# Attention and a shrink layer on one core: output turned by PE transposes, the band mask as a sum in PSUM, DMA turns from pair 10, and a re-costed planner

## The chip, the cores and the metric

The kernel runs on one core of one Trainium2 chip. The metric is device time in microseconds (us) of one execution; the kernel before has a median of 334.55 us over 13 runs, from 331.03 to 338.65 us. The engines are PE (TensorE: matmuls, with its weight loads shown as PEld), DVE (VectorE), ACT (ScalarE), POOL (GpSimd) and SP (SyncE, which here only issues DMAs). Each engine executes its own instructions in the order in which they were emitted, and waits at an instruction whose inputs are not there.

## The reference

Inputs are q, k and v of shape (batch 8, heads 8, sequence 576, depth 64) and two weights, w_in (512 x 2048) and w_out (2048 x 512). For each batch and head two attentions are added:

```
local: softmax(q k^T / 8, only where |i - j| < 4) v
pooled: q, k, v averaged over groups of 4 tokens (144 groups),
        softmax(qd kd^T / 8) vd, each row repeated 4 times
x = (local + pooled), heads joined: 4608 tokens x 512
h = x w_in;  g = h - tanh(h);  out = g w_out
```

## The kernel before

**Attention by pairs.** The 64 (batch, head) items are taken two heads at a time: 32 pairs, four pairs (NP = 4) to a batch. A pair's q and k come by DMA into `qkn` (four buffers), v windows into `vst`. They are cast to bf16 and interleaved into `qr` (L515, L523), and turned so that depth lies on the partitions, into `qk`. Up to pair 11 the turn is nine PE transposes (L547) with copies out of PSUM (L551); from pair 12 (`T_DMA`) it is one DMA transpose `qT<-qr` (L531) and an ACT copy (L534). Pooled q and k are sums of four columns (`half` L564, `qkd` L569). From pair 12 (`NEW`) pooled v comes from its own load `v4` and two POOL sums (L472, L476); before that from PE (L492, L494).

**Scores and band.** The local scores are computed in windows: a tile of 120 queries against the 128 keys around it, four tiles and a last one of 96, so that a pair has 2 x 480 scores in one two-bank PSUM piece `t1` (L584), and 2 x 96 plus the pooled scores (L606) in another, `t2`. ACT takes the exponentials into `E` (L622, L634, L637). For pairs 0 to 3 PE adds a bias of -32768 outside the band before the scores (L589). For pairs 4 to 31 DVE multiplies the exponentials in SBUF by a 0/1 `mask` (L626 for 960 columns, L641 for 192). Then PE multiplies by v (L650, L657; a column of ones gives the sums), and DVE normalises into `ln` (L670, L672): seven blocks of up to 128 rows, five local and two pooled.

**Turn of the output.** `ln` must be turned so that heads lie on partitions, and pooled rows repeated 4 times. Up to pair 11 PE does both in one sum (`back`, L683 to L692): matmuls of the pooled blocks with a 0/1 matrix `up` and of the local blocks with the identity, into two PSUM banks, copied to `xT` by DVE (L720) or ACT (L721). From pair 12 (`X_DMA`) one DMA transpose `lT<-ln` (L696) turns it, and DVE or POOL (`join`, L703 and L709) adds local and repeated pooled part in SBUF.

**Dense part.** The 4608 tokens are nine blocks of 512. For each, `mm1` makes 16 tiles of h (L734, 4 matmuls of 512 columns each), ACT takes tanh (L742) and DVE subtracts (L745) into `gT`; `mm2` makes four tiles of the output (L760, 16 matmuls each), ACT copies them to `y` (L771) and SP stores them (L774). Block b needs all pairs of the batches that its tokens lie in.

**What sets the order.** A planner inside the kernel (`Program`) writes the order out. Each operation is entered with an engine, or several to choose from, a cost in ns, what it reads and writes, and a priority. `order` plays a list schedule with these costs: the engines, a latency `LAT` after each, 16 DMA queues as one resource, and eight PSUM banks with a cap for each kind of use (`P.cap`: attention "b" 6 banks, dense "d" 4). The instructions are then emitted in the order of the starts found, so the costs decide which instruction stands behind which on each engine. The chip waits only for data; where `after=` names a key, it is a dependence of the planner's order alone. `load_next` issues the loads of pair p + 4 in step p.

Of the kernel before, what the change touches and what calls it, by code (L numbers as in the profile page):

```python
# [23 lines left out]
class Program:  # L24

    LAT = {"PE": 270, "ACT": 150, "DVE": 110, "POOL": 150, "SP": 50, "DMA": 2200}
    RING = 230

    def __init__(self):
        self.ops = []  # L30
        self.alternatives = {}
        self.slack = []
        self.soon = set()
        self.goal = set()
        self.ring = {}
        self.rings = {}
        self.touch = []
        self.use = []
        self.toks = []
        self.cap = {}  # L40
        self.last_write = {}
        self.readers = {}
# [66 lines left out]
    def order(self):  # L109
# [56 lines left out]
        for i in range(n):  # L166
            if left[i] == 0:
                make_ready(i)
        for step in range(n):
            best = None  # L170
            for eng, cand in ready.items():
                if not cand:
                    continue
                now = max(free.get(eng, 0.0), min(at[i] for i in cand))
                if eng == "PE":
# [8 lines left out]
                else:  # L184
                    pick = min((self.ops[i][4], i) for i in cand if at[i] <= now)[1]
# [12 lines left out]
            end = now + self.ops[i][1]  # L198
            want = [t for t in self.use[i] if t.first == i]
# [57 lines left out]
def kernel(  # L257
# [41 lines left out]
    mask = fixed("mask", [128, 576], BF16)  # L299
# [19 lines left out]
    up = lT[1].rearrange("p n c -> p (n c)")[:, 0:S]  # L319
    r = fixed("r", [128, 2, 7], FP32, 2)  # L320
    ln = fixed("ln", [128, 7, 128], BF16, 2)
# [31 lines left out]
    def c_up():  # L353

        GP.memset(up, 1.0)
        GP.affine_select(out=up, in_=up, compare_op=ALU.is_ge, fill=0.0,
                         base=0, pattern=[[1, S]], channel_multiplier=-4)
        GP.affine_select(out=up, in_=up, compare_op=ALU.is_ge, fill=0.0,
                         base=3, pattern=[[-1, S]], channel_multiplier=4)

# [8 lines left out]
    def c_mask():  # L369

        GP.memset(mask, 1.0)
        m4 = mask[:, 0:480].rearrange("p (t c) -> p t c", c=QW)
        for part, pat in ((m4, [[0, 4], [1, QW]]),
                          (mask[:, 480:576], [[1, 96]])):
            neg = [[-s, n] for s, n in pat]
            GP.affine_select(
                out=part, in_=part, compare_op=ALU.is_ge, fill=0.0,
                base=-1, pattern=neg, channel_multiplier=1)
            GP.affine_select(
                out=part, in_=part, compare_op=ALU.is_ge, fill=0.0,  # L380
                base=7, pattern=pat, channel_multiplier=-1)
        GP.affine_select(
            out=mask[:, 0:QW], in_=mask[:, 0:QW], compare_op=ALU.is_ge,
            fill=0.0, base=-4, pattern=[[0, QW]], channel_multiplier=1)
        GP.affine_select(
            out=mask[:, 480:576], in_=mask[:, 480:576], compare_op=ALU.is_ge,
            fill=0.0, base=99, pattern=[[0, 96]], channel_multiplier=-1)
# [6 lines left out]
    def load_qk(p):  # L394

        b, h0, s = p // NP, 2 * (p % NP), p % NQKN
        for i, src in enumerate((q, k)):
# [6 lines left out]
            load(600, issue, [("qkn", s, i)], T_QK, 380, -30, 8, (), eng)  # L404
# [63 lines left out]
    def pool_v4(p):  # L468
# [9 lines left out]
        op("POOL", 1150, a1, reads=[("v4", s)], writes=["v2"], pri=10 * p - 12)  # L478
        op("POOL", 750, a2, reads=["v2"], writes=[("vp", s)], pri=10 * p - 12)

    def pool_v(hb):
# [15 lines left out]
        op("ACT", 590, lambda: A.copy(  # L497
# [5 lines left out]
    def attention(p):  # L503
# [10 lines left out]
        if p >= NEARLY:  # L514
            op("POOL", 1300, lambda: GP.tensor_copy(  # L515
# [14 lines left out]
        if p >= T_DMA:  # L530
            P.dma("SP", 1740, lambda: nc.sync.dma_start_transpose(  # L531
                out=qT[s], in_=qr[s].rearrange("p a c -> p (a c)")), 1300, 72,
                  src=[("qr", s, 0), ("qr", s, 1)], dst=[("qT", s)], pri=-50, lead=500)
            op("ACT", 1250, lambda: A.copy(  # L534
# [3 lines left out]
        else:  # L538
            for a0, a1, tn, cn in ((0, 5, 290, 740), (5, 9, 230, 620)):
# [10 lines left out]
                def copy(fn, a0=a0, a1=a1, b16=b16):  # L550
# [5 lines left out]
                          ("DVE", cn, lambda copy=copy: copy(V.tensor_copy))][:1 + (p < NP)],  # L556
# [10 lines left out]
        def add2(eng):  # L567
            with nc.allow_low_precision("pooled q and k"):
                eng.tensor_tensor(out=qkd[s][:, 0:G],  # L569
                                  in0=half[:, :, 0, :],  # L570
                                  in1=half[:, :, 1, :], op=ALU.add)
        P.choice([(name, n1, lambda eng=eng: add1(eng)) for name, n1, _, eng in adders],
# [41 lines left out]
        if new:  # L614
            op("PE", 620, s12, slack=late, reads=qks + [("qkd", s)], fill=[t1, t2], pri=pri)
        else:
            op("PE", 420 * cold + 250 * (p < NP), s1, slack=late,
# [4 lines left out]
        op("ACT", 960, lambda: A.activation(  # L622
            out=e1, in_=two(t1)[:, :, 0:480], func=AF.Exp, scale=SCALE),
           drain=[t1], writes=[("E", e, 0)], pri=pri)
        if p >= NP:
            op("DVE", 950, lambda: V.tensor_tensor(  # L626
                out=e1, in0=e1,
                in1=mask[:, 0:480].unsqueeze(1).to_broadcast([128, 2, 480]),
                op=ALU.mult), reads=["mask"], writes=[("E", e, 0)], pri=pri)
        yield  # L630
        if not new:
            op("PE", 380 * cold + 100 * (p < NP), s2, slack=late, reads=qks + [("qkd", s)],
               fill=[t2], pri=pri)
        op("ACT", 310, lambda: A.activation(  # L634
            out=e2v, in_=two(t2)[:, :, 0:96], func=AF.Exp, scale=SCALE),
           drain=[t2], writes=[("E", e, 1)], pri=pri)
        op("ACT", 650, lambda: A.activation(  # L637
            out=e3, in_=two(t2)[:, :, 96:384], func=AF.Exp, scale=SCALE / 16.0),
           drain=[t2], writes=[("E", e, 2)], pri=pri)
        if p >= NP:  # L640
            op("DVE", 450, lambda: V.tensor_tensor(  # L641
                out=e2v, in0=e2v,
                in1=mask[:, 480:576].unsqueeze(1).to_broadcast([128, 2, 96]),
                op=ALU.mult), reads=["mask"], writes=[("E", e, 1)], pri=pri)
# [25 lines left out]
        op("DVE", 200, lambda: V.reciprocal(out=r[s], in_=blocks()[:, :, :, 64]),  # L670
           drain=[to], writes=[("r", s)], pri=pri)
        op("DVE", 1060, lambda: V.tensor_tensor(  # L672
# [6 lines left out]
        tb = P.psum(2, kind)  # L679
# [72 lines left out]
    def mm2(kb, i):  # L752
        ts, part, g = i // 4, i % 4, kb % 2
        if part == 0:
            ycur[0] = P.psum(1, "d")
# [189 lines left out]
```

The softmax here doesn't subtract the row's maximum and nothing guards it: scores larger than these inputs give would overflow.

## Time and profile before

| what | us |
|---|---|
| median of 13 runs | 334.55 |
| the profiled execution, whole | 336.22 |
| its span in the profile | 334.2 |
| first matmul of the dense part (L734) | 26.47 |
| last pair's `xT` written (L709) | 251.5 |
| end of the last matmul | 329.85 |

So 2.0 us of the profiled execution lie outside the span, and that execution was 1.7 us above the median. In the views, a line number is a line of the kernel before; "busy" of a matmul is a modelled length (379 ns for 512 columns, though such matmuls start every 216 ns), so steps from start to start are read where an exact cost is needed. The waits view names for an instruction the engine that released it.

### The profile page before, as it was taken

The page shows a single profiled execution, that of the slowest core. Times are in us where ns is not written, and L with a number is a line of the kernel's source. Part 1 is how long each engine was busy: PE and PEld are TensorE (multiplying, and loading weights), DVE is VectorE, ACT ScalarE, POOL GpSimd, SP SyncE. Part 2 cuts the span into 40 slices and gives each one's busy share as a digit, 9 for nine tenths or more (in the row PEclk, how much of TensorE's full clock was granted, in tenths as well). Part 3 has the DMA queues.
Part 4 walks back from the last instruction along what each step waited for, and adds up shares of the span by engine and source line. Part 5 has one row for each costly group of instructions (what it writes and reads, how often), then busy time and mean ns, then how long its engine had stood idle before and what let it go on. Part 6 is the DMA issues. An engine that isn't in the chain of part 4 may idle for free.

```text
span 334.2 us, 6546 instructions
## 1 busy us (share of the span) xinstructions
PE 317.9 (95%) x2461; PEld 158.9 (48%) x2461; DVE 214.1 (64%) x330; ACT 202.7 (61%) x334; POOL 178.5 (53%) x211
## 2 busy tenths in 40 slices
PE   6889999999999999999897999999999999999994
PEld 2554454655444444444443444445444444444441
DVE  4777864577966969787979868757763344433300
ACT  2977853589778766687865476877544444444411
POOL 7754647869667698979987848887310000000000
PEclk9999999999999999999999999999999999999999
DMA  7999999999999999999999999982320001000021
GB/s 223 263 223 211 239 252 264 291 290 118 306 215 261 234 237 261 232 270 234 241 249 228 272 225 282 193 187 61 90 59 33 31 31 65 31 31 31 33 94 64
DMA packets 108862, 59.80 MB, mean 179 GB/s; under 512 B 86174, under 2 KB 96030, under 8 KB 108830
## 3 DMA queue, kind: packets, MB, share of 16 engines
q1 hardware_dynamic: 104318, 54.60, 71.4%
q0 software_dynamic: 4224, 4.19, 7.6%
q10 hardware_dynamic: 288, 0.59, 0.6%
q8 instruction: 19, 0.31, 0.4%
q14 instruction: 13, 0.11, 0.1%
HBM read 43.64 MB, written 9.44 MB: 159 GB/s over the span
## 4 chain that ended last, share of the span: by engine, by line
PE 72%; DVE 11%; DMA 9%; ACT 2%; issue 2%; SPq 1%; POOL 1%; POOLq 0%; DVEq 0%; ACTq 0%
PE bank L760 31%; PE bank L734 29%; DMA qkn<-in_k_dram 6%; DVE E L626 3%; DMA lT<-ln 3%; PE bank L650 2%; PE bank L584 2%; DVE ln L672 2%; PE bank L657 2%; DVE gT L745 2%; DVE E L641 1%; DVE xT L709 1%; ACT E L622 1%; PE bank L547 1%; DVE xT L703 1%
## 5 line engine op out<-in xcount | busy, mean ns | idle before, releaser
L734 PE MATMUL bank<-xT,w_in_sb 128*128 128x512 bf16 x576 | 146.0, 379 | 0.3 <-DVE gT L745 0.3
L760 PE MATMUL bank<-w_out_sb,gT 128*128 128x512 bf16 x576 | 145.2, 379 | 0.0
L745 DVE TENSOR_TENSOR gT<-bank,u 128x512 bf16<-128x512 f32 x144 | 97.5, 686 | 63.5 <-ACT u L742 63.0
L742 ACT ACTIVATE u<-bank 128x512 f32<-128x512 f32 x144 | 85.9, 598 | 79.4 <-PE bank L734 76.7
L760 PEld LDWEIGHTS <-gT 128*128 128x128 bf16 x576 | 53.9, 98 | 61.9
L734 PEld LDWEIGHTS <-w_in_sb 128*128 128x128 bf16 x576 | 53.9, 98 | 61.8 <-issue 0.5
L564 POOL TENSOR_TENSOR half<-qk 128x576 f32<-128x576 bf16 x28 | 32.1, 1147 | 21.1 <-ACT qk L551 11.1
L626 DVE TENSOR_TENSOR E<-E,mask 128x960 bf16<-128x960 bf16 x28 | 31.9, 1141 | 11.9 <-ACT E L622 11.9
L622 ACT ACTIVATE E<-bank 128x960 bf16<-128x960 f32 x32 | 31.1, 973 | 12.8 <-PE bank L584 12.7
L515 POOL CAST qr<-qkn 128x1152 bf16<-128x1152 f32 x28 | 33.0, 1178 | 8.0 <-DMA qT<-qr 4.5
L672 DVE TENSOR_TENSOR ln<-bank,r 128x896 bf16<-128x896 f32 x32 | 34.7, 1087 | 0.9
L771 ACT COPY y<-bank 128x512 f32<-128x512 f32 x36 | 21.1, 587 | 18.7 <-PE bank L760 18.3
L451 POOL CAST vw<-vst 128x640 bf16<-128x640 f32 x31 | 25.8, 837 | 7.3 <-DMA vst<-in_v_dram 7.2
L472 POOL TENSOR_TENSOR v<-v 72x512 f32<-72x512 f32 x20 | 25.5, 1273 | 2.3 <-DMA v<-in_v_dram 1.5
L534 ACT COPY qk<-qT 128x1152 bf16<-128x1152 bf16 x20 | 24.1, 1204 | 0.4 <-DMA qT<-qr 0.3
L650 PE MATMUL bank<-vw,E 128*128 128x65 bf16 x320 | 20.1, 194 | 3.9 <-DVE E L641 3.0
L476 POOL TENSOR_TENSOR vp<-v 72x256 bf16<-72x256 f32 x20 | 14.5, 726 | 16.2 <-PE bank L657 16.1
L569 POOL TENSOR_TENSOR qkd<-half 128x288 bf16<-128x288 f32 x29 | 21.5, 741 | 1.9 <-DVE r L670 0.9
L650 PEld LDWEIGHTS <-E 128*128 128x128 bf16 x320 | 16.5, 98 | 11.1 <-DVE E L641 3.5
L637 ACT ACTIVATE E<-bank 128x576 bf16<-128x576 f32 x32 | 21.1, 659 | 0.0
L641 DVE TENSOR_TENSOR E<-E,mask 128x192 bf16<-128x192 bf16 x28 | 18.2, 651 | 0.9 <-ACT E L634 0.9
L703 POOL TENSOR_TENSOR xT<-lT 128x480 bf16<-128x480 bf16 x11 | 11.4, 1035 | 12.7 <-DMA lT<-ln 12.5
(75 smaller groups left out, 223.9 us busy)
## 6 DMA issues: line engine op xcount, KB each, us to landing
vst<-in_v_dram SPq DMA_DIRECT2D x62, 160.0 KB, 4.8
qkn<-in_q_dram SPq DMA_DIRECT2D x32, 288.0 KB, 5.3
out_dram<-y SPq DMA_DIRECT2D x36, 256.0 KB, 4.8
qkn<-in_k_dram SPq DMA_DIRECT2D x30, 288.0 KB, 7.0
v<-in_v_dram SPq DMA_DIRECT2D x20, 288.0 KB
w_in_sb<-in_moe_w_in_dram POOLq DMA_DIRECT2D x4, 512.0 KB, 12.6
w_out_sb<-in_moe_w_out_dram POOLq DMA_DIRECT2D x4, 512.0 KB, 9.9
qkn<-in_k_dram ACTq DMA_DIRECT2D x2, 288.0 KB, 3.1
```

Of the source, the lines that this page charges most:

```text
L451: P.choice([(eng, ns, lambda fn=fn: fn(out=vw[w][:, 2 * jj:2 * jj + 2, :, 0:64], in_=vst[s])) for eng, ns, fn in CAST_V[p >= NEARLY]], rea ...
L472: GP.tensor_tensor(out=v2, in0=v4[s][:, :, :, 0:128], in1=v4[s][:, :, :, 128:256], op=ALU.add)
L515: op("POOL", 1300, lambda: GP.tensor_copy(out=qr[s].rearrange("p a (h d) -> p h a d", h=2), in_=qkn[sn].rearrange("p h (a d) -> p h a d", ...
L564: eng.tensor_tensor(out=half, in0=four[:, :, 0:2, :], in1=four[:, :, 2:4, :], op=ALU.add)
L622: op("ACT", 960, lambda: A.activation(out=e1, in_=two(t1)[:, :, 0:480], func=AF.Exp, scale=SCALE), drain=[t1], writes=[("E", e, 0)], pri=pri)
L626: op("DVE", 950, lambda: V.tensor_tensor(out=e1, in0=e1, in1=mask[:, 0:480].unsqueeze(1).to_broadcast([128, 2, 480]), op=ALU.mult), reads= ...
L650: T.matmul(two(to)[:, hh, 65 * t:65 * t + 65], E[e][:, c:c + 128], vw[w][:, 2 * jj + hh, t, :], start=True, stop=True)
L672: op("DVE", 1060, lambda: V.tensor_tensor(out=ln[s].rearrange("p n (h d) -> p h n d", d=D), in0=blocks()[:, :, :, 0:64], in1=r[s].unsqueez ...
L734: T.matmul(one(tok), w_in_sb[:, dc, fc * 128:(fc + 1) * 128], xT[dc][:, kb * 512:kb * 512 + 512], start=(dc == 0), stop=(dc == N_DC - 1))
L742: op("ACT", 590, lambda: A.activation(out=u[us], in_=one(tok), func=AF.Tanh), drain=[tok], writes=[("u", us)], pri=DPRI)
L745: op("DVE", 670, lambda: V.tensor_tensor(out=gT[g][:, fc, :], in0=one(tok), in1=u[us], op=ALU.subtract), drain=[tok], reads=[("u", us)], w ...
L760: T.matmul(one(tok), gT[g][:, fc, ts * 128:ts * 128 + 128], w_out_sb[:, fc, :], start=(fc == 0), stop=(fc == N_FF - 1))
```

## The change

1. **Output up to pair 9.** `back` becomes seven PE transposes into one bank in bf16. The pooled part is copied to a small tile `od` (DVE or ACT), and one DVE sum adds local part and repeated `od` into `xT`. `up` and its three POOL instructions go.
2. **DMA turns two pairs earlier.** `T_DMA` and `X_DMA` go from 12 to 10. `join` is left to POOL alone.
3. **Band.** For pairs 4 to 31 DVE adds the -32768 bias to the scores in PSUM before the exponential, in place of multiplying the exponentials in SBUF. `mask` goes; `bias` is made directly by POOL.
4. **Loads.** In the planner, q and k of pair p wait for the DMA turn of pair p - 3, where that pair is 10 or later (`BACK`).
5. **Merged scores** (local and pooled in one PE operation) from pair 8, not 12 (`MERGE`).
6. **Dense part.** `mm2` has PSUM banks of its own kind, "y", cap 3, beside "d", 4. The last output tile is made in two halves of 256 columns, each copied and stored by itself.
7. **Planner.** Most costs and `LAT` are changed; POOL and the DVE's pooling sums (`P.port`) are modelled as excluding each other; the cast of v may go to ACT for all pairs.

The diff, cut to its core:

```diff
-    LAT = {"PE": 270, "ACT": 150, "DVE": 110, "POOL": 150, "SP": 50, "DMA": 2200}
+    LAT = {"PE": 235, "ACT": 145, "DVE": 110, "POOL": 140, "SP": 50, "DMA": 2000}
...
+                if eng == "DVE":
+                    now = max(free.get(eng, 0.0), min(
+                        max(at[i], port) if i in self.port else at[i] for i in cand))
+                elif eng == "POOL":
+                    now = max(now, port)
...
+            if eng == "POOL" or eng == "DVE" and i in self.port:
+                port = end
...
-        if new:
-            op("PE", 620, s12, slack=late, reads=qks + [("qkd", s)], fill=[t1, t2], pri=pri)
+        if p >= MERGE:
+            op("PE", 590, s12, slack=late, reads=qks + [("qkd", s)], fill=[t1, t2], pri=pri)
...
+        def band(tok, lo, hi):
+            part = two(tok)[:, :, 0:hi - lo]
+            V.tensor_tensor(out=part, in0=part, in1=bias[:, lo:hi].unsqueeze(1)
+                            .to_broadcast([128, 2, hi - lo]), op=ALU.add)
+        if p >= NP:
+            op("DVE", 1080, lambda: band(t1, 0, 480), reads=["bias"], fill=[t1], pri=pri)
+        op("ACT", 860, lambda: A.activation(
             out=e1, in_=two(t1)[:, :, 0:480], func=AF.Exp, scale=SCALE),
...
         if p >= NP:
-            op("DVE", 950, lambda: V.tensor_tensor(
-                out=e1, in0=e1,
-                in1=mask[:, 0:480].unsqueeze(1).to_broadcast([128, 2, 480]),
-                op=ALU.mult), reads=["mask"], writes=[("E", e, 0)], pri=pri)
...
+            op("DVE", 280, lambda: band(t2, 480, 576), reads=["bias"], fill=[t2], pri=pri)
...
-        tb = P.psum(2, kind)
+        tb = P.psum(1, kind)
+
+        def flat():
+            return one(tb).bitcast(BF16)[:, 0:S + G]
 
         def back():
...
+            for t in range(7):
+                q0, n = (QW * t, NQ[t]) if t < NT else (S + 128 * (t - NT), (128, 16)[t - NT])
+                T.transpose(flat()[:, q0:q0 + n], ln[s][0:n, t, :], ident[0:n, 0:n])
...
-            P.choice([("DVE", 1900, lambda: join(V)), ("POOL", 1400, lambda: join(GP))],
+            P.choice([("POOL", 1310, lambda: join(GP))],
                      reads=[("lT", s)], writes=[("x", b, j)], pri=pri)
...
-        xs = xT[j][:, b * S:(b + 1) * S].rearrange("p (n c) -> p n c", n=2)
-        P.choice([("DVE", 720, lambda: V.tensor_copy(out=xs, in_=two(tb)[:, :, 0:288])),
-                  ("ACT", 680, lambda: A.copy(out=xs, in_=two(tb)[:, :, 0:288]))],
-                 drain=[tb], writes=[("x", b, j)], pri=pri)
+        P.choice([("DVE", 130, lambda: V.tensor_copy(out=od[s], in_=flat()[:, S:S + G])),
+                  ("ACT", 170, lambda: A.copy(out=od[s], in_=flat()[:, S:S + G]))],
+                 drain=[tb], writes=[("od", s)], pri=pri)
+        op("DVE", 610, lambda: V.tensor_tensor(
+            out=xT[j][:, b * S:(b + 1) * S].rearrange("p (g a) -> p g a", a=4),
+            in0=flat()[:, 0:S].rearrange("p (g a) -> p g a", a=4),
+            in1=od[s].unsqueeze(2).to_broadcast([128, G, 4]), op=ALU.add),
+           drain=[tb], reads=[("od", s)], writes=[("x", b, j)], pri=pri)
...
-        op("DVE", 670, lambda: V.tensor_tensor(
+        op("DVE", 610, lambda: V.tensor_tensor(
             out=gT[g][:, fc, :], in0=one(tok), in1=u[us], op=ALU.subtract),
...
+        split = kb == NBLK - 1 and ts == 3
+        if split:
+            cols, first, fcs = 256 * (part // 2), part % 2 == 0, 8
+        else:
+            cols, first, fcs = 0, part == 0, 4
+        if first:
+            ycur[0] = P.psum(1, "y")
...
-    M2_FIRST, T_DMA, X_DMA, NEW, LATE = 16, 12, 12, 12, 0
+    M2_FIRST, T_DMA, X_DMA, NEW, LATE = 16, 10, 10, 12, 0
+    MERGE = 8
+    BACK = 3
...
-    CAST_V = [[("POOL", 820, GP.tensor_copy), ("ACT", 640, A.copy)],
-              [("POOL", 820, GP.tensor_copy)]]
+    CAST_V = [[("POOL", 770, GP.tensor_copy), ("ACT", 620, A.copy)],
+              [("POOL", 770, GP.tensor_copy), ("ACT", 620, A.copy)]]
...
-            load_qk(nl[0])
+            t = nl[0] - BACK
+            load_qk(nl[0], [("qT", t % 2)] if t >= T_DMA else ())
...
-    P.cap = {"b": 6, "d": 4}
+    P.cap = {"b": 6, "d": 4, "y": 3}
```

## The prediction

> **What bounds the kernel now.** I read the page first (busy times, slices, chain of waits).
>
> ```profile
> PE 317.9 (95%) x2461; PEld 158.9 (48%) x2461; DVE 214.1 (64%) x330; ACT 202.7 (61%) x334; POOL 178.5 (53%) x211
> PE   6889999999999999999897999999999999999994
> DVE  4777864577966969787979868757763344433300
> POOL 7754647869667698979987848887310000000000
> DMA  7999999999999999999999999982320001000021
> PE 72%; DVE 11%; DMA 9%; ACT 2%; issue 2%; SPq 1%; POOL 1%; POOLq 0%; DVEq 0%; ACTq 0%
> ```
>
> PE is the bound, and the dense part alone is 1152 matmuls x 0.216 = 248.8 us. DMA is full to slice 27 but carries only 9% of the chain. So time can go in four places: the head before the dense part (26.5 us), PE's attention work, PE's idle time, and the tail (329.85 to 334.2). The stage view finds the idle time:
>
> ```profile
> 70.00:160.00 90.00, 88.95 (x756) 44.94 (x755) 72.62 (x103) 67.76 (x112) 70.98 (x77) 1.00 1.16 238
> 160.00:190.00 30.00, 26.44 (x241) 13.53 (x238) 27.19 (x36) 18.75 (x31) 25.36 (x29) 1.00 1.16 244
> 190.00:236.00 46.00, 45.37 (x355) 22.20 (x354) 34.02 (x52) 32.63 (x53) 34.18 (x38) 1.00 0.86 188
> ```
>
> Columns: window, length, then busy PE, PEld, DVE, ACT, POOL. In 160:190 PE misses 3.56 us, with DVE at 27.2 of 30. As modelled matmuls overlap, I also summed, from 27 us on, each step between matmul starts beyond its own length (216 ns for 512 columns, 56 for 128, 29 to 33 for 65): 16.2 us. About 4.7 of it are steps of some 95 ns wherever PE changes between row heights (33 times before scores alone). The rest are waits. The groups by shape say what they are:
>
> ```profile
> L745 DVE TENSOR_TENSOR gT<-bank,u 128x512 bf16<-128x512 f32 x144 | 97.5, 686 | 63.5 <-ACT u L742 63.0
> L672 DVE TENSOR_TENSOR ln<-bank,r 128x896 bf16<-128x896 f32 x32 | 34.7, 1087 | 0.9
> L626 DVE TENSOR_TENSOR E<-E,mask 128x960 bf16<-128x960 bf16 x28 | 31.9, 1141 | 11.9 <-ACT E L622 11.9
> L641 DVE TENSOR_TENSOR E<-E,mask 128x192 bf16<-128x192 bf16 x28 | 18.2, 651 | 0.9 <-ACT E L634 0.9
> L703 DVE TENSOR_TENSOR xT<-lT 128x480 bf16<-128x480 bf16 x9 | 11.7, 1298 | 1.3 <-DMA lT<-ln 1.3
> ```
>
> By line, L626 takes 0.64 to 3.48 us, L641 0.24 to 3.80, while L745 and L672, whose first input is PSUM, never pass 0.69 and 1.09. The stretched ones have both inputs in SBUF. The timeline shows on what:
>
> ```profile
> 178.56 3.80 DVE L641 TENSOR_TENSOR E<-E,mask 128x192 bf16<-128x192 bf16 x1
> 178.53 1.01 POOL L703 TENSOR_TENSOR xT<-lT 128x480 bf16<-128x480 bf16 x1
> 179.50 0.35 POOL L709 TENSOR_TENSOR xT<-lT 128x96 bf16<-128x96 bf16 x1
> 179.79 1.38 POOL L451 CAST vw<-vst 128x640 bf16<-128x640 f32 x2
> 181.12 1.15 POOL L515 CAST qr<-qkn 128x1152 bf16<-128x1152 f32 x1
> 182.43 0.20 PE L650 MATMUL bank<-vw,E 128*128 128x65 bf16 x1 [1.54 <-DVE E L641]
> ```
>
> A 0.24 us product waits until POOL's unbroken run ends at 182.27; PE stands behind it. The Trainium skill ("SBUF — State Buffer", section "Who interferes with whom") has this lock, but says the holder keeps the ports for one instruction. That would cap each wait at POOL's longest, 1.27 us; this row shows 3.56 over five. By the rule the stalls at 161.9 and 182.3 would be other things, and the gain below 2.3 us smaller (325.6).
>
> **The change, part by part.**
>
> *Band in PSUM.* The new sums have one PSUM input, like L745 and L672, which nothing stretches. From these two, one element costs (1087 - 686)/384 = 1.04 ns, so 960 take 1.15 us and 192 take 0.35. For 28 pairs: 42.1 us of DVE against 50.1. Beside a silent POOL a pair gets 0.62 us longer (1.50 against 0.89), and `t1` keeps its banks 1.15 us more; dense matmuls lie over that, and if they don't, it costs up to 28 x 0.62 = 17 us. The stalls of PE behind stretched DVE work are, by starts: 0.46 (72.7 us), 0.41 (86.7), 0.67 (130.1), 0.56 (161.9), 0.85 (165.7), 1.70 (180.7), 0.32 (187.3), 0.79 (207.3), and 0.41 of the wait for a stretched `qkd` at 177.6: 6.2 us. Next late is ACT's last exponential, which was early. Bounds: 0 (another wait follows) to -11.5 (all idle but the 4.7). I take **-6.2**.
>
> *Joins.* DVE loses nine (18.6 us); POOL gets them and two more, 11 x 1.46 = 16 us. Its late pair costs 0.73 + 1.15 + 1.15 + 0.67 + 1.27 + 0.73 + 1.36 (join) = 7.1 us; exponentials of pairs 12 to 31 come every 7.6. Casts can go to ACT. Cover: the last `xT` is there at 251.5, and behind it PE needs only `mm2` of block 7 and block 8, 41.5 us before 329.85, so attention may be 36.8 us late, 1.9 per pair. Nothing.
>
> *PE work.* An output turn and a q,k turn, by starts:
>
> ```profile
> 58.38 0.67 PE L547 MATMUL bank<-ident,qr 128*128 128x128 bf16 x9
> 58.88 0.59 PE L760 MATMUL bank<-w_out_sb,gT 128*128 128x512 bf16 x2
> 61.67 0.41 PE L683 MATMUL bank<-lT,ln 128*128 128x288 bf16 x2
> 62.41 1.46 PE L760 MATMUL bank<-w_out_sb,gT 128*128 128x512 bf16 x6
> ```
>
> `back` takes 0.745 us, nine transposes 0.50, so 56 ns each. Seven of up to 128 columns: 0.34 by columns, 0.45 with a 16-row step as at L685 (0.13); I take 0.40, saving 0.345. Pairs 4 to 7: block 0's last matmul is at 69.5 and block 1's first at 70.2, just behind pair 7's `xT` (68.0), so PE may only wait in that time: half of 1.4, **-0.7** (0 to -1.4). Pairs 8, 9: **-0.7**. Pairs 10, 11 lose both turns: 2 x 1.25 = **-2.5**. Merging scores (0.32 + 0.28 against 0.50) in pairs 8 and 9: **-0.2**. The split last tile: 32 x 0.113 (a 256-column matmul, L492) against 16 x 0.216: **+0.2**. Together **-3.9**.
>
> *DMA and SP.* Four more DMA turns, 5.2 (`qT`) and 4.6 us (`lT`) from issue to landing, on full queues at 74 to 110 us; each also occupies SP some 1.3 us and waits there for `qr` or `ln` with loads queued behind it. `BACK` adds no wait on the chip, it only puts loads behind turns. Loads land in 5 to 7 us, under one pair's 7.6, with four buffers. Covered by the 36.8 us; uncovered, 4 x 5 = 20 us once. Nothing.
>
> *DVE and ACT at the output.* For pairs 0 to 9, a sum of 576 (0.75) and a copy of 144 (about 0.30, same line) replace one copy (0.76 or 0.64): off PE's path but for the head.
>
> *Head.* Three `back`s lie on the chain (20.1 to 21.7, 25.1 to 26.0): -1.0; the extra copy adds about 0.4 before the first dense matmul. The input loads (6.5 us of DMA before 11.3) stay. **-0.5** (-1.0 to +0.4). `up`'s 1.9 us of POOL lie beside waits for loads: nothing.
>
> *"y" banks.* Waits of dense matmuls are 0.3 us in the groups: nothing.
>
> *Tail.* The last copy falls from 0.587 to about 0.39 us (between 0.335 for 192 and 0.587 for 512 elements); the last store's packets run 0.8 us, half of that goes. **-0.6** (0 to -0.6).
>
> **Sum:** -6.2 - 3.9 - 0.5 - 0.6 = -11.2. The profiled execution's 336.22 becomes 325.0; it lay 1.7 above the median, so 334.55 becomes **323.3**.
>
> **The rivals.**
> A, *other waits take the lock's place*: PE executes in order, every start moves with the new costs, and waits for POOL's `qkd` or ACT arise. For: two `qkd` waits today (0.82, 0.94). Against: only L626, L641, L703 and L709 vary much. -11.2 + 6.2 = -5.0: 329.5.
> B, *most waits go*: with steady durations the planned order holds and only the 95 ns steps stay: -11.5 for -6.2, 318.0. For: the planner's costs are single numbers, and the varying operations leave. Against: waits for loads at 49.6 us.
> C, *slower: POOL is late for `qkd`*. POOL at 7.1 of 7.6 us makes each late pair's scores wait for L569 with PE blocked, 0.94 as at 177.6: 20 x 0.94 = +18.8, 342.2. It decides from 0.56 us per pair on. Against: casts may move to ACT, and DVE no longer stretches POOL (L569 0.67 to 1.08).
> D, *it does nothing*: PE's idle time only moves. Pairs 4 to 7, which wait for loads, hold up block 1, and the lock's 6.2 and PE's 3.9 come back as waits: -11.2 + 10.1 = -1.1, 333.5.
>
> **How the numbers follow.** Forecast 0.45, A 0.22, B 0.20, C 0.09, D 0.04. The range 315.5 to 332.5 takes in the bounds of the terms, A and most of B, and leaves out C, D and B's far side. A measurement here can tell about 0.5% (1.7 us) from no change: faster 0.84 (forecast, B, nearly all of A), same 0.06, slower 0.10.
>
> **What would show it.** Right: the band sums at 1.15 and 0.35 us with no spread; L650 no longer waiting for DVE; missing PE time in 160:190 under 1.5 us; `back` near 0.40; the dense part starting near 26; 0.6 us less behind the last matmul. Wrong: new idle before L606 or L584 (C), the same 16 us of idle under other names (A), or a dense part that starts late.

## The result and the profile after

The changed kernel takes 338.98 us (median of 11 runs, 336.39 to 341.61) against 334.59 us (48 runs of the kernel before): ratio 1.0146, interval 1.0113 to 1.0178. It is **1.5% slower**; the forecast was 323.3 us, and the range ended at 332.5. All ratios here are of fast executions alone, without those in which the same kernel ran over 1.5% above its fastest, so they are not quite the ratios of the medians. The profiled execution took 338.98 us, the median, with a span of 337.3; that of the kernel before lay 1.7 us above its median, so the two spans differ by 3.1 us only, where the medians differ by 4.4.

The page of the kernel after, busy times, slices and chain of waits:

```profile
PE 315.8 (94%) x2418; PEld 158.7 (47%) x2418; DVE 192.4 (57%) x318; ACT 205.7 (61%) x347; POOL 173.7 (51%) x217
PE   6889999999988997988999989899999999999995
DVE  5587875389834875567586755676733334444400
POOL 5493526837869796779788879876110000000000
DMA  7999999969999999999999999983240000100022
PE 65%; DMA 15%; ACT 5%; POOL 4%; issue 4%; DVE 3%; SPq 3%; ACTq 0%; POOLq 0%; DVEq 0%
```

DVE has 21.7 us less to do and POOL 4.8 less (it gets all the joins, but 16 casts of v went to ACT). But DMA's share of the chain went from 9% to 15%, ACT's from 2% to 5% and POOL's from 1% to 4%, while DVE's fell from 11% to 3%. The stage view (window, length, then busy PE, PEld, DVE, ACT, POOL) says where:

```profile
70.00:160.00 90.00, 81.85 (x676) 40.74 (x675) 60.37 (x95) 64.53 (x106) 69.03 (x79) 1.00 1.09 236
160.00:190.00 30.00, 28.55 (x253) 14.78 (x251) 19.30 (x31) 22.75 (x39) 24.25 (x28) 1.00 1.06 246
190.00:236.00 46.00, 43.08 (x360) 21.37 (x356) 29.76 (x45) 32.19 (x52) 36.72 (x45) 1.00 0.96 211
```

In 160:190, the window from which the forecast was made, PE now misses 1.45 us where it missed 3.56: the repair works there. In 70:160 it misses 8.15 us (before 1.05), and in 190:236 2.92 (before 0.63). Summed by starts from 27 to 240 us, as for the kernel before, PE's idle time is 23.4 us against 16.2. So the span's +3.1 us is +7.2 of idle time, -0.9 in the tail, +0.1 at the dense part's start, and what remains, -3.3, must be work taken off PE.

The waits view of the kernel after, with engine, line, operand, what it waited for, us in total, times, longest (rows left out between are marked):

```profile
ACT vw L452 <- DMA vst<-in_v_dram: 15.8, 9, 3.4
...
POOL v L473 <- DMA v<-in_v_dram: 8.7, 12, 2.1
ACT qk L535 <- DMA qT<-qr: 8.6, 6, 2.9
...
POOL vw L452 <- DMA vst<-in_v_dram: 6.6, 6, 2.8
...
PE bank L731 <- DVE gT L742: 3.6, 3, 1.9
```

The same view of the kernel before has no wait of ACT for a v load (POOL made 31 of the 32 casts), and for `qT` this:

```profile
ACT qk L534 <- DMA qT<-qr: 0.3, 1, 0.3
```

Now ACT stands 24.4 us for loads of v and for `qT`, and ACT also makes the tanh that PE needs. (POOL's joins waited long for `lT` before, 12.5 us, and wait 15.9 now.) One such stop, from the timeline (start, length, engine, line; in brackets the idle time before it and its releaser):

```profile
144.73 1.66 SPq L532 DMA_TRANSPOSE qT<-qr  x1
...
150.42 1.16 ACT L535 COPY qk<-qT 128x1152 bf16<-128x1152 bf16 x1 [2.94 <-DMA qT<-qr]
...
151.49 1.08 ACT L739 ACTIVATE u<-bank 128x512 f32<-128x512 f32 x2
...
152.11 1.29 DVE L742 TENSOR_TENSOR gT<-bank,u 128x512 bf16<-128x512 f32 x2 [2.83 <-ACT u L739]
...
152.86 0.59 PE L731 MATMUL bank<-xT,w_in_sb 128*128 128x512 bf16 x2 [1.95 <-DVE gT L742]
```

The copy `qk<-qT` stands in ACT's order ahead of a tanh whose input has long been there. The turn lands late, the copy waits 2.94 us, the tanh with it, DVE with the tanh, and PE 1.95 us: it waits for a PSUM bank, which the subtraction on DVE has to give back. What comes late is one transfer; the order of ACT's instructions passes the delay on to work that does not need the transfer.

**Plan against chip.** The planner's own starts can be written out beside the trace. I call *slip* the start of each tanh on the chip less its planned start. The kernel after was planned to end at 317.3 us, the kernel before at 323.8: the planner expected 6.5 us of gain. Slip in us at times of the chip:

| at us | 30 | 100 | 120 | 160 | 190 | 240 |
|---|---|---|---|---|---|---|
| before | -1.1 | 2.5 | 2.5 | 3.0 | 7.5 | 7.8 |
| after | 1.4 | 1.5 | 5.7 | 11.8 | 14.1 | 17.9 |

Planned end and last slip make 331.6 and 335.2, 2.6 and 2.1 short of the spans, so this table holds the difference between the kernels to within half a microsecond. The kernel after keeps its plan up to its last tanh before 100 us, which starts at 86.8 (the slip stays between 0.8 and 1.8 us); then it loses 16.4 us. It was planned to turn out a late pair every 6.91 us and gets one every 7.66; before, 7.31 was planned and 7.60 came. (The expectations below give 9.2 and 16.1 us for the two kernels' loss from 30 to 240 us, where this table has 8.9 and 16.5; no reading hangs on that.)

### The profile page after: what moved, and what is told of

Same layout as the page of the kernel before. It is cut to its first block, busy times and chain, and to the rows that moved or that the text cites. A ratio compares the mean times of both kernels' runs of the same rounds, so it can differ in the third digit from the quotient of the medians.

```text
span 337.3 us, 6513 instructions
## 1 busy us (share of the span) xinstructions
PE 315.8 (94%) x2418; PEld 158.7 (47%) x2418; DVE 192.4 (57%) x318; ACT 205.7 (61%) x347; POOL 173.7 (51%) x217
## 4 chain that ended last, share of the span: by engine, by line
PE 65%; DMA 15%; ACT 5%; POOL 4%; issue 4%; DVE 3%; SPq 3%; ACTq 0%; POOLq 0%; DVEq 0%
PE bank L764 29%; PE bank L731 26%; DMA vst<-in_v_dram 5%; DMA v<-in_v_dram 3%; DMA lT<-ln 3%; PE bank L586 3%; ACT u L739 2%; DMA qkn<-in_q_dram 2%; PE bank L650 2%; DMA qT<-qr 2%; PE bank L657 2%; PE bank L548 1%; SPq L532 1%; DVE ln L672 1%; DVE gT L742 1%
## 5 line engine op out<-in xcount | busy, mean ns | idle before, releaser
L731 PE MATMUL bank<-xT,w_in_sb 128*128 128x512 bf16 x576 | 143.5, 379 | 4.1 <-DVE gT L742 3.6
L742 DVE TENSOR_TENSOR gT<-bank,u 128x512 bf16<-128x512 f32 x144 | 97.4, 688 | 87.0 <-ACT u L739 86.8
L764 PE MATMUL bank<-w_out_sb,gT 128*128 128x512 bf16 (+1 forms) x592 | 143.1, 374 | 0.0
L764 PEld LDWEIGHTS <-gT 128*128 128x128 bf16 x592 | 55.5, 98 | 60.6
L626 DVE TENSOR_TENSOR bank<-bank,bias 128x960 f32<-128x960 f32 (+1 forms) x56 | 41.5, 758 | 13.7 <-PE bank L586 11.3
L776 ACT COPY y<-bank 128x512 f32<-128x512 f32 (+1 forms) x37 | 21.4, 578 | 20.6 <-PE bank L764 20.5
L535 ACT COPY qk<-qT 128x1152 bf16<-128x1152 bf16 x22 | 26.7, 1212 | 9.7 <-DMA qT<-qr 8.6
L696 POOL TENSOR_TENSOR xT<-lT 128x480 bf16<-128x480 bf16 x22 | 22.2, 1010 | 16.0 <-DMA lT<-ln 15.9
L650 PE MATMUL bank<-vw,E 128*128 128x65 bf16 x320 | 20.1, 194 | 2.0 <-ACT E L639 0.7
L452 ACT CAST vw<-vst 128x640 bf16<-128x640 f32 x16 | 11.8, 740 | 15.8 <-DMA vst<-in_v_dram 15.8
L650 PEld LDWEIGHTS <-E 128*128 128x128 bf16 x320 | 16.3, 98 | 9.3 <-ACT E L630 1.8
L586 PE MATMUL bank<-qk 64*128 64x120 bf16 (+1 forms) x320 | 15.6, 216 | 2.4 <-ACT E L630 2.1
L586 PEld LDWEIGHTS <-qk 64*128 64x128 bf16 x320 | 9.5, 95 | 16.3 <-issue 10.2
```

The source lines that it names most:

```text
L535: op("ACT", 1095, lambda: A.copy(out=full.rearrange("p (g a) i -> p g a i", a=A9), in_=qT[s].rearrange("p a (g i) -> p g a i", i=2)), read ...
L586: T.matmul(two(tok)[:, hh, c:c + NQ[t]], qk[s][rows, k0:k0 + 128, 1], qk[s][rows, q0:q0 + NQ[t], 0], start=p >= NP, stop=p >= NP or t >= 3)
L626: V.tensor_tensor(out=part, in0=part, in1=bias[:, lo:hi].unsqueeze(1) .to_broadcast([128, 2, hi - lo]), op=ALU.add)
L650: T.matmul(two(to)[:, hh, 65 * t:65 * t + 65], E[e][:, c:c + 128], vw[w][:, 2 * jj + hh, t, :], start=True, stop=True)
L731: T.matmul(one(tok), w_in_sb[:, dc, fc * 128:(fc + 1) * 128], xT[dc][:, kb * 512:kb * 512 + 512], start=(dc == 0), stop=(dc == N_DC - 1))
L742: op("DVE", 610, lambda: V.tensor_tensor(out=gT[g][:, fc, :], in0=one(tok), in1=u[us], op=ALU.subtract), drain=[tok], reads=[("u", us)], w ...
```

## The experiments

Theory (called here *late loads*): after 100 us, loads and turns land later than the planner's order assumes, and engines stand at them in order. Rivals: POOL or PSUM sums as such are too slow; two more pairs of DMA turns are too many; the planner's costs alone are wrong; the stretched DVE products were never worth 6 us. Ratios are to executions of the kernel before from the same round (medians of 333.75 to 335.11 us), with their intervals. "Same order" means that the planner's entries are untouched, so only the chip's durations change.

**Less to load, same order.** `e1_light` is the kernel after with lighter loads from pair 8, `e5_light_before` the same edit on the kernel before; `e13_light_v` and `e14_light_qk` are the kernel after with one kind each.

```diff
+                nh = 1 if p >= 8 else 2
...
-                    out=qkn[s][i::2], in_=src[b, h0:h0 + 2].rearrange(
+                    out=qkn[s][i::2, 0:nh], in_=src[b, h0:h0 + nh].rearrange(
...
+                    nw = 2 if p >= 8 else 5
-                    nc.sync.dma_start(out=t[:, i], in_=win(-4, 128, 5))
+                    nc.sync.dma_start(out=t[:, i, 0:nw], in_=win(-4, 128, nw))
...
+            nv = 2 if p >= 14 else 4
...
```

> The kernel after with the same planned order, in which the loads carry less: from pair 8 on q and k bring one head of two, v two windows of five, and from pair 14 on the pooled v half its rows; what is not loaded keeps older data, so this part of the computation is left out. In the kernel after, the dense matmuls start up to 17.8 us later than the planner's order has them; the slip grows from 1.9 us at 91 us to 17.8 at 216 us, and the chain of waits there names loads and DMA turns. Theory 1 (loads and turns land later than planned, and ACT and POOL stand in order behind them): the slip after 91 us shrinks to under 6 us, and the time falls by 8 to 14 us, to 325 to 331. Theory 2 (the band sums in PSUM, or the PSUM banks that they hold, block PE): loads don't matter, 337 to 340. Theory 3 (the order is unlucky in a way that has to do with neither): 335 to 340.

> The kernel before, its planned order unchanged, with the light loads of the first experiment (from pair 8 one head of two of q and k, two windows of five of v; from pair 14 half the pooled v; that part of the computation is left out). Before slips 9.2 us behind its plan between 30 and 240 us. The prediction gave 6.2 us of PE's waits to DVE products stretched by POOL; light loads do not touch that. If that is right, the slip stays near 6 and the time falls by 2 to 4 us, to 330 to 333. If late loads make nearly all of the slip in before as well, it falls under 2.5 us, and the time to 325 to 328.

> The kernel after with only v's window loads light (two windows of five from pair 8; that part of v is left out). Light q, k, v and pooled v together took the slip from 16.1 us to 0.2. These windows were 27.6 of the 58 us of packet time that went (16 engines together). If ACT's casts of v, which wait 15.8 us for these loads, carry the delay: slip under 4 us, 323 to 328. If the full DMA queues do, whatever the load: about half, slip 6 to 10 us, 328 to 333.

> The kernel after with only the loads of q and k light (one head of two from pair 8; that part is left out), 19.3 of the 58 us of packet time. If ACT's casts of v carry the delay: slip 13 to 16 us, 336 to 339. If the full DMA queues do: slip 8 to 12 us, 330 to 335.

| kernel | us | ratio | slip, 30 to 240 us |
|---|---|---|---|
| after | 338.98 | 1.0146 [1.0113, 1.0178] | 1.4 to 17.9 |
| `e1_light` | 322.40 | 0.9662 [0.9608, 0.9715] | 0.8 to 1.6 |
| `e13_light_v` | 328.14 | 0.9785 [0.9689, 0.9880] | 0.3 to 8.0 |
| `e14_light_qk` | 328.00 | 0.9814 [0.9718, 0.9910] | 1.4 to 6.3 |
| `e5_light_before` | 336.24 | 1.0045 [1.0006, 1.0083] | -1.6 to 7.8 |

With lighter loads the chip executes the new plan almost to the microsecond. The waits that are left of those above, in `e1_light` (POOL's for `lT` stays, 13.3 us, and the plan is kept beside it):

```profile
POOL vw L454 <- DMA vst<-in_v_dram: 0.9, 2, 0.5
...
POOL v L476 <- DMA v<-in_v_dram: 0.6, 1, 0.6
```

and its stage view:

```profile
70.00:160.00 90.00, 88.97 (x759) 45.68 (x770) 65.78 (x103) 72.93 (x119) 77.73 (x90) 1.00 0.86 183
160.00:190.00 30.00, 29.50 (x241) 15.12 (x245) 22.43 (x35) 23.29 (x39) 27.18 (x33) 1.00 0.85 197
```

POOL, DVE and ACT do more per microsecond than in the kernel after and next to nothing is late, so no engine is too slow for the plan. Either kind of load alone brings back about eleven microseconds: it is not one kind of transfer that is late, but whatever shares the queues and SP's order. (Lighter q and k alone did more than either theory expected of them: 330 us at best.) And the kernel before gains nothing from light loads: what delays it is not its loads, or not its loads alone.

**The stretched products.** `e9_one_input` is the kernel before, with each of the two mask products replaced by a DVE operation on one SBUF input at the same place (a maximum over an axis of length 1; the mask is left out); `e12_one_light` adds the light loads.

```diff
-            op("DVE", 950, lambda: V.tensor_tensor(
-                out=e1, in0=e1,
-                in1=mask[:, 0:480].unsqueeze(1).to_broadcast([128, 2, 480]),
-                op=ALU.mult), reads=["mask"], writes=[("E", e, 0)], pri=pri)
...
+                    V.tensor_reduce(out=e1, in_=e1.unsqueeze(3), op=ALU.max,
+                                    axis=mybir.AxisListType.X)
...
+            op("DVE", 950, sum1, reads=["mask"], writes=[("E", e, 0)], pri=pri)
```

> The kernel before, plan and order unchanged, in which each of the mask's two products is replaced by a DVE instruction of the same shape with one SBUF input, in place (a maximum over an axis of length 1); so the mask for pairs 4 to 31 is left out. Each new instruction waits for the same exponentials and holds up the same matmuls. The prediction's claim (PE lost 6.2 us to products that POOL's SBUF traffic stretched): no such instruction over 1.2 us, the slip behind the plan falls from 9.2 us to 2 to 4 (the joins in SBUF stay), the time to 327 to 331. Rival (the slip of before has another source): slip 7 to 10, 333 to 336.

> The kernel before with both edits at once, its plan and order unchanged: light loads as in e5_light_before and one-input DVE instructions in place of the mask's products as in e9_one_input (so the mask, and the same parts of q, k and v, are left out). Light loads alone changed nothing (slip 9.7 us), the one-input instructions alone took 2.4 us off the slip. If the two are parallel delays, each hidden behind the other: slip 0 to 3 us and 323 to 329. If the rest of the slip has a third source (the joins in SBUF, or the planned order itself): slip 5 to 7 us, 329 to 333.

`e9_one_input`: 332.70 us, 0.9968 [0.9931, 1.0006], slip -2.2 to 4.7. `e12_one_light`: 329.81 us, 0.9845 [0.9760, 0.9931], slip -1.3 to 2.0. The groups by shape of `e9_one_input`:

```profile
L628 DVE TENSOR_REDUCE E<-E 128x960 bf16<-128x960 bf16 x28 | 32.1, 1147 | 10.7 <-ACT E L622 10.5
L705 DVE TENSOR_TENSOR xT<-lT 128x480 bf16<-128x480 bf16 x9 | 11.1, 1228 | 7.8 <-DMA lT<-ln 7.8
L644 DVE TENSOR_REDUCE E<-E 128x192 bf16<-128x192 bf16 x28 | 9.6, 342 | 2.3 <-ACT E L635 2.3
```

The 28 long ones lie between 1.13 and 1.15 us and the short ones between 0.33 and 0.35, where the products ran from 0.24 to 3.80: with one SBUF input nothing is stretched, which the Trainium skill states as a rule for such DVE instructions ("SBUF — State Buffer", section "Who interferes with whom"). But the waits view of the same kernel now has these, beside 12.5, 1.3 and 0.3 us in the kernel before:

```profile
POOL xT L705 <- DMA lT<-ln: 18.1, 8, 7.5
...
DVE xT L705 <- DMA lT<-ln: 7.8, 6, 2.6
...
ACT qk L534 <- DMA qT<-qr: 5.3, 5, 1.5
```

So the kernel before holds **two delays, one behind the other**: stretched products, and late loads and turns. Light loads alone: nothing. Unstretched products alone: about 1 us, with an interval that reaches no change, and a slip of 6.9 us, between what theory and rival had. Both: 4.8 us below the kernel before's 334.6, and slip grows by 3.3 instead of 8.9 us. That is just outside the 0 to 3 expected, and where the 3.3 come from was not looked for.

**The band sums alone, and who casts v.** `e4_band_only` puts only the band in PSUM into the kernel before (t1's and t2's sums with the new costs, no products); `e3_pool_casts` takes ACT off the late v casts of the kernel after.

```diff
+            op("DVE", 1080, lambda: band(t1, 0, 480), reads=["bias"], fill=[t1], pri=pri)
...
-            op("DVE", 950, lambda: V.tensor_tensor(
-                out=e1, in0=e1,
-                in1=mask[:, 0:480].unsqueeze(1).to_broadcast([128, 2, 480]),
-                op=ALU.mult), reads=["mask"], writes=[("E", e, 0)], pri=pri)
```

```diff
-              [("POOL", 770, GP.tensor_copy), ("ACT", 620, A.copy)]]
+              [("POOL", 770, GP.tensor_copy)]]
```

> The kernel before, with one part of the change alone: the band is a sum in PSUM ahead of the exponential (the mask's two products in SBUF are gone, their planner costs replaced by 1080 and 280); all other costs and settings are those of before, the computation is whole. The prediction's theory (PE's idle time behind stretched DVE products, 6.2 us, goes): 326 to 331, and no DVE sum over 1.2 us. Rival (the band in PSUM holds banks and delays exponentials, which costs as much): 334 to 338. A reordering of chance would give anything between 331 and 338.

> The kernel after, in which the cast of v for pairs 4 to 31 may go to POOL alone, as before; the computation is whole. After has 16 such casts on ACT, which wait 15.8 us for v's loads, with tanh queued behind them. Theory 1a (ACT's queue behind these casts is what stops PE): ACT waits for v's loads no more, PE's waits for tanh and for exponentials shrink, 331 to 335. Rival (POOL gets 16 x 0.72 us more and becomes late for the pooled q and k): 339 to 344, with new idle time of PE ahead of L608. If load lateness just moves to POOL's queue: 337 to 341.

`e4_band_only`: 336.53 us, 1.0105 [1.0033, 1.0177]; its plan already ends 3.0 us later (326.8), and DVE's joins wait 16.5 us for `lT` (1.3 before). The time lies in the rival's range, and by the planner's own costs the sums ahead of the exponentials do cost those 3.0 us in this order; so this run does not show the 6.2 us gain, nor does it part the rival from late turns. That the sums need not hold anything up is shown by `e1_light`, which has them all and keeps its plan. `e3_pool_casts`: 342.00 us, 1.0254 [1.0179, 1.0330]. ACT no longer waits for v, but this row replaces the 8.6 us:

```profile
ACT qk L535 <- DMA qT<-qr: 25.3, 13, 3.1
```

The wait moved from one late transfer to another. That the casts' new engine is the cause falls. The rival has a part: PE's waits for `qkd` grow from 2.0 to 4.0 us.

**The planner's DMA costs.** `e2_dma_costs` is the kernel after with the DMA latency and costs of the kernel before, `e6_before_low` the reverse. The diff is that of `e2_dma_costs`. `e8_fit_dma` is the kernel after with transfer costs fitted to the packets' times in the trace (second diff); `e10_fit_sp` adds to it the time for which SP's turn instructions were seen to run (`qT` 1340 to 2000, `lT` 1260 to 1600), and `e11_fit_lat` to that the old latency of 2200.

```diff
-    LAT = {"PE": 235, "ACT": 145, "DVE": 110, "POOL": 140, "SP": 50, "DMA": 2000}
+    LAT = {"PE": 235, "ACT": 145, "DVE": 110, "POOL": 140, "SP": 50, "DMA": 2200}
...
-            P.dma("SP", 1340, lambda: nc.sync.dma_start_transpose(
+            P.dma("SP", 1740, lambda: nc.sync.dma_start_transpose(
...
-            P.dma("SP", 1260, lambda: nc.sync.dma_start_transpose(
+            P.dma("SP", 1350, lambda: nc.sync.dma_start_transpose(
...
-            P.dma("SP", 440, lambda: nc.sync.dma_start(
+            P.dma("SP", 530, lambda: nc.sync.dma_start(
...
-    T_QK, T_V, T_W, W_PRI, NEARLY = 760, 850, 3000, 32, NP
+    T_QK, T_V, T_W, W_PRI, NEARLY = 800, 1000, 2850, 32, NP
```

```diff
-        load(520, issue, [("v4", s)], 900, 184, -30, 18)
+        load(520, issue, [("v4", s)], 1115, 184, -30, 18)
...
-                out=qT[s], in_=qr[s].rearrange("p a c -> p (a c)")), 1300, 72,
+                out=qT[s], in_=qr[s].rearrange("p a c -> p (a c)")), 1530, 72,
...
-                out=lT[s], in_=ln[s].rearrange("p n c -> p (n c)")), 1000, 72,
+                out=lT[s], in_=ln[s].rearrange("p n c -> p (n c)")), 1190, 72,
...
-    T_QK, T_V, T_W, W_PRI, NEARLY = 760, 850, 3000, 32, NP
+    T_QK, T_V, T_W, W_PRI, NEARLY = 810, 850, 3000, 32, NP
```

> The kernel after, in which only the planner's costs that concern DMA are those of before: 2200 for the latency of a DMA, 800 and 1000 for the loads of q or k and of v, 2850 for weights, and SP's costs of a turn and of a store. Nothing else changes, the computation is whole. Theory 1 (the lower DMA costs make the order expect loads too early): the slip behind the plan falls and the time goes to 331 to 336. Theory 2 (band sums): unchanged within 2 us of 339. Theory 3 (the loads are late because of the two more pairs of DMA turns, not because of the costs): within 2 us of 339.

> The kernel before, in which only the planner's DMA costs are those of after: 2000 for the latency of a DMA, 760 and 850 for loads of q or k and of v, 3000 for weights, 1340, 1260 and 440 for SP. The plan's late pairs then come every 6.4 us in place of 7.3; the chip gave 7.6 in both kernels. The computation is whole, no other part of the change is in. Theory 1 (an order that expects a pair sooner than DMA can bring it makes PE wait): the late pairs still come every 7.5 to 7.9 us, the slip grows by 15 to 25 us, and the time to 340 to 350. If the costs are harmless and other parts of the change made it slow: 333 to 337.

> The kernel after with the planner's DMA costs fitted to the trace: from the time that the packets took, 16 engines together, divided by 1.13 for their overlap, a load of q or k costs 810, of v 850, of pooled v 1115, a turn of q and k 1530, of the output 1190. The plan's late pairs then come every 7.65 us, the chip's own pace. The computation is whole, nothing else changes. Theory 1: the slip between 30 and 240 us falls from 16.1 to under 5 us, ACT's waits for v's loads under 5 us, and the time is 323 to 330, faster than both kernels. Rival (two more pairs of turns, or the band in PSUM, cost what after lost): 335 to 340.

> The kernel after with the fitted DMA costs of e8, and besides SP's cost of a DMA turn as the trace of after has it: 2000 for q and k (median 2.08 us) and 1600 for the output (mean 1.54), in place of 1340 and 1260. The computation is whole. After e8 the plan still slipped 9.9 us. If what is missing is SP's queue, which stands in its turns while the DMA queues are full: slip under 5 us, 323 to 329. If the size of the slip does not depend on SP's costs: within 2 us of e8, 331 to 335.

> e10 with, besides, the planner's DMA latency of before, 2200 in place of 2000. The computation is whole. If the fit of e10 is what matters, within 2 us of e10. If latency is what the plan lacks: 2 to 4 us faster than e10, with shorter waits of ACT for v's loads and for the turned q and k.

| kernel | planned end | slip, 30 to 240 us | us | ratio |
|---|---|---|---|---|
| `e2_dma_costs` | 320.5 | -1.5 to 10.7 | 334.46 | 0.9990 [0.9944, 1.0036] |
| `e6_before_low` | 325.0 | -1.9 to 16.4 | 346.01 | 1.0371 [1.0313, 1.0429] |
| `e8_fit_dma` | 318.7 | -0.6 to 9.3 | 332.78 | 0.9963 [0.9928, 0.9997] |
| `e10_fit_sp` | 318.2 | -1.8 to 10.2 | 334.43 | 0.9969 [0.9904, 1.0034] |
| `e11_fit_lat` | 318.5 | -0.9 to 12.2 | 334.87 | 0.9986 [0.9940, 1.0032] |

The costs alone move the kernel by 11 us in one direction (before to `e6_before_low`) and by 4.5 to 6.2 in the other (after to `e2_dma_costs` and `e8_fit_dma`), with the same work done. So the lower DMA costs are a cause of the loss. In `e6_before_low` the late pairs came every 7.16 us, not every 7.5 to 7.9 as expected, but the slip grew by 18.3. They are not all of it: with fitted costs 9.9 us of slip remain, and ACT still waits 12.5 us for v and 13.8 for `qT` in `e8_fit_dma`. My theory that fitting every cost to the trace would bring the slip to nothing fell with `e10_fit_sp` and `e11_fit_lat`, which gave nothing more (their traced executions lie 2.1 us below and 2.3 above their medians, so their slips are rough). `e8_fit_dma` is the only complete kernel of the study with a ratio clear of 1 on the fast side, by 0.4% of the kernel before, with an interval that nearly touches 1; out of several tries that may be chance.

**Two smaller rivals.** `e7_turns12` is the kernel after with the DMA turns from pair 12 again; `e15_store_act` issues its output stores from ACT, to take them off SP.

```diff
-    M2_FIRST, T_DMA, X_DMA, NEW, LATE = 16, 10, 10, 12, 0
+    M2_FIRST, T_DMA, X_DMA, NEW, LATE = 16, 12, 12, 12, 0
```

```diff
-            P.dma("SP", 440, lambda: nc.sync.dma_start(
+            P.dma("ACT", 440, lambda: nc.scalar.dma_start(
```

> The kernel after with the DMA turns from pair 12 again, not 10 (T_DMA and X_DMA 12), the rest as in after; the computation is whole. The plan's late pairs come every 6.3 us. Rival (the four more DMA turns overload the queues): 333 to 336. Theory 1 (what counts is how far the planned pace is ahead of DMA's 7.6 us per late pair, and that is further here): no faster than after, 338 to 346.

> The kernel after with the output stores issued from ACT's queue, not SP's, in the plan as well; bytes and packets stay the same, the computation is whole. SP is busy or waiting 127 of the 135 us from 90 to 225 us. If SP's queue (its issues in order, loads behind waiting turns) is what delays the loads: slip 6 to 11 us, 329 to 335. If the DMA engines are: slip 13 to 18 us, 336 to 341.

`e7_turns12`: 338.88 us, 1.0143 [1.0087, 1.0199], no different from the kernel after. Its plan ends 3.2 us later (320.5) and slips from -0.8 to 14.8: the two pairs turned earlier win in the plan and nothing on the chip, but they are not what makes it slower. `e15_store_act`: 342.84 us, 1.0234 [1.0160, 1.0307]: the stores on SP are not what makes the turns late, or ACT loses more by them. The Trainium skill ("DMA: Bandwidth & Descriptors", section "Issuing engines are not separate DMA queues") says that another issuer saves only the issue time; that run does not speak against it.

**What stays open.** The loads are not slow once issued: the packets of q and k loads in 90 to 225 us have landed 3.7 us (median) after their issue, where the planner put 4.7 and its latency of 2.0 behind that. They are issued late. From 90 to 225 us SP's DMA instructions run for 124 of the 135 us (122 in the kernel before), and for 106 in `e1_light`; a `qT` turn takes a median of 2.08 us there (2.02 in the kernel before, planned 1.34), and 1.35 in `e1_light`. So SP was as full before the change. Whether SP's instruction or the 16 engines behind it is the place that fills up was not separated, since light loads relieve both. Raising SP's planned cost gave nothing, which speaks against SP's time alone. Nor is it one rate that the queues can't pass: late pairs came every 7.66 us in the kernel after, but every 7.04 in `e7_turns12`, 7.16 in `e6_before_low` and 8.15 in `e10_fit_sp`, and a shorter pace did not make a shorter time. What of the full queues the planner's model lacks is not settled. Two rivals were not run alone. One is `BACK`, which puts loads behind turns in SP's order; it cannot be needed for the slip, since `e6_before_low` slips 18.3 us without it, but it may have a share in what the kernel after lost. The other is chance: any new cost reorders the whole plan, and the complete variants of the kernel after lie from 332.78 to 342.84 us; how far a plan's time moves by that alone was not measured.

## Why the prediction was wrong

**The step that failed is "DMA and SP"**: "Covered by the 36.8 us; uncovered, 4 x 5 = 20 us once. Nothing." The 36.8 us are real as slack of the last `xT` against the end. But an engine with other work behind the wait cannot use them: each executes a fixed order, and ACT's late `qT` copies and v casts stand in it between the tanhs of the dense part. In the stop shown above a wait of 2.94 us for a turn cost PE 1.95 us there and then, however much slack that pair has at the end. The same step priced the added DMAs, four turns (`e7_turns12`: no difference), and not the planner's lower DMA costs, which moved the loads and turns of all 20 late pairs: a pair was now planned every 6.91 us (7.18 with the old DMA costs, `e2_dma_costs`), where the kernel before had got one every 7.60. `e6_before_low` prices those costs at +3.7% by themselves, on the kernel before. The step also read a turn's hold on SP too low: "some 1.3 us" fits `lT` (median 1.26 us in the kernel before), but a `qT` turn held SP for a median of 2.15 us there, and up to 5.41.

**Lock, -6.2.** The mechanism held: the sums in PSUM have no spread (0.36 to 1.17 us over both lengths), L650 no longer waits for DVE, and 160:190 misses under 1.5 us. All three were named as signs of being right, and they came true in a slower kernel, since they look at the repaired place alone. The size did not hold: without the stretching the kernel before gains about 1 us, as late turns stand right behind. Where loads are light as well, it is worth 6.4 (336.24 to 329.81), the size that I had. Rival A named the step ("other waits take the lock's place"), but with POOL's `qkd` or ACT's work as the new wait; it was DMA, and rival A kept the other savings. (POOL's longest instruction was 1.54 us, not 1.27, which changes nothing in the argument on the lock.)

**Rival B** (most waits go, -11.5) rests on 4.7 us of steps at a change of row height. The kernel before has 82 such steps between 27 and 240 us, of 92 to 102 ns, 7.8 us in all; so real waits were some 8.5 us, and B was priced about 3 us too high. In the kernel after 72 such steps make 6.7 us, so its real waits are some 16.7 us, twice as much.

**Rival C** (slower: POOL late for `qkd`, 342.2) had the sign and nearly the time, but not the cause: PE's waits for `qkd` come to 2.0 us (1.4 before).

**The rest of the sum.** Groups by shape and steps of the kernel after:

```profile
L626 DVE TENSOR_TENSOR bank<-bank,bias 128x960 f32<-128x960 f32 x28 | 32.4, 1158 | 11.4 <-PE bank L586 11.3
L626 DVE TENSOR_TENSOR bank<-bank,bias 128x192 f32<-128x192 f32 x28 | 10.0, 357 | 2.3 <-PE bank L608 2.2
```

```profile
57.08 0.59 PE L687 MATMUL bank<-ident,ln 120*128 120x120 bf16 x7
57.60 0.61 PE L764 MATMUL bank<-w_out_sb,gT 128*128 128x512 bf16 x2
```

- Band sums: 1.16 and 0.36 us against 1.15 and 0.35, 42.4 us together against 42.1. Right.
- `back`: 0.52 us from start to start, not 0.40; it saves 0.23 per pair, not 0.345. By starts it holds a step of 0.11 us for the 16 rows, for which I had allowed, and one of 0.15 us at a change of row height, for which I had not.
- PE work -3.9: -3.3 by the difference above, not measured by itself.
- Head -0.5: the dense part starts at 26.56 us, before at 26.47. Nothing. What PE saves there is gone by then.
- Tail -0.6: 337.3 - 333.84 = 3.46 us behind the last matmul, before 4.35. -0.9, beyond the bound of -0.6.
- Joins and POOL, 0: right for POOL, whose long join sums take 1.01 us each (1.04 before). "Casts can go to ACT" came true for 16 of them, and the step had no price for what ACT then waits: 15.8 us for loads of v.
- "y" banks, 0: the 3.6 us for which dense matmuls now wait for a bank come from DVE's late subtractions (`e1_light` has no such wait), so nothing speaks against it.

The work that the change removes is there to be had: with light loads the kernel after is 13.8 us below the kernel before with light loads (322.40 against 336.24; by the ratios of the two rounds 3.8%, or 12.8 us), beside 11.2 forecast. With full loads all of it, and 4.4 us more, is lost behind late DMA.

## What to carry to other kernels

Slack at the end of a chain is cover only for an engine that has nothing else to do: where engines execute a fixed order, ask of each late transfer which instruction stands behind its consumer. Where a planner writes that order, put its planned starts beside the trace first; where the slip grows is where the chip does not follow its costs, and a plan with tighter costs can lose time by them alone. Where two delays may lie one behind the other, remove each alone and both together before saying what either is worth.

## What the runs showed of the hardware

- SP's DMA transpose instruction is not of one length: from 90 to 225 us `qT<-qr` took a median of 2.08 us in the kernel after and 1.35 us with lighter loads, at the same places in SP's order (2.02 and 1.31 in the kernel before and in `e5_light_before`).
- In the kernel after, packets of 256 bytes (of several kinds, not separated) took 24 ns each on average and of 2304 bytes 114 ns, so the large ones carried 1.9 times the bytes per unit of time. The 256-byte packets are 127.6 us of the 16 engines' time, more than twice the 58.1 us of the q and k loads.
- A DVE maximum over an axis of length 1 took 1.147 us for 960 elements of bf16, as the sum in PSUM did (1.158), with no spread beside a busy POOL.
- A change of row height between two matmuls cost PE 92 to 102 ns beyond the matmul's own length, up or down (82 times between 27 and 240 us of the kernel before).
